# Two attention blocks on one core: narrower guard products, strided scaling, and new due times for the projection jobs

## The chip, the cores and the metric

The kernel runs on one core of a Trainium2 chip. The metric is the device time of the whole program in microseconds (us). The engines are TensorE (PE in the profile, PEld for its weight loads), VectorE (DVE), ScalarE (ACT), GpSimd (POOL) and SyncE (SP, which issues most DMAs). SBUF is the working memory; PSUM takes the matmuls' outputs, in 8 banks of 512 float32 columns for each of 128 partitions.

## What is computed

There are two independent attention blocks over 2048 tokens of width 1024, with 32 heads of 32 channels each. Their outputs stand side by side in an output of 2048 x 2048. Inputs and output are bfloat16.

Block A is plain attention:

```
q, k, v = split(A_x @ A_wqkv)                       # 32 heads x 2048 x 32
p = softmax(q @ k.T / sqrt(32));   a = (p @ v) @ A_wo
```

Block B cuts the tokens into 4 segments of 512. In each segment it mixes causal attention inside the segment with a linear memory of the segments before, by a gate for each head:

```
q, k, v = B_x @ B_wq, B_x @ B_wk, B_x @ B_wv        # 4 segments x 512 tokens
for s in range(4):
    a_dot = softmax(q[s] @ k[s].T / sqrt(32) + causal mask) @ v[s]
    a_mem = phi(q[s]) @ M / (phi(q[s]) . z + 1e-6)  # phi(t) = t + 1 if t > 0 else exp(t)
    o[s] = g * a_mem + (1 - g) * a_dot              # g = sigmoid(beta), one per head
    M += phi(k[s]).T @ v[s];   z += sum(phi(k[s]))
b = o @ B_wo
```

## The kernel before

**Attention.** Heads are worked four at a time: a group g is 4 heads of A (8 groups), and B has 8 such groups j in each segment s, taken in pairs (s, 0) to (s, 3). A unit is 256 query columns of a group of A, or a pair of groups of B. `plan_set` (line 911) writes the logits of four heads into two of three PSUM slots of two banks each (`SLOT_BANKS`): one matmul for each head and 128 keys (line 955). `plan_exp` (1003) lets ACT take the exponential of 1024 logits a partition into a ring of 20 buffers (`P_RING`; line 1034). `round` (1096) multiplies the probabilities by V and by a column of ones (1130 and 1137, the PV rounds), into one accumulator bank. `norm` (1178) turns the sums into reciprocals by `recip_rows` (1144): a 32x32 transpose (1155) brings the sums of a head into one column of every 32, a reciprocal is taken (1165), for B it is scaled by 1 - g (1167), and a second transpose (1169) spreads it again. B's memory denominators go through the same function with 1e-6 added (1162) and a reciprocal in place (1163). For about a quarter of A's key tiles the exponential of one tile in four is a cubic on DVE and POOL instead (`plan_cube`, 979: lines 992, 995, 996, 997).

**Guards.** The exponentials subtract no maximum. Instead a bound on each unit's logits is computed from sums of squares. POOL squares the projected keys and queries (`square`, 1314); `guard_cols` (1321) sums the squares of each head over its channels by a matmul (1327), 512 tokens wide, and takes the maximum over the tokens (1334); `guard_end` (1365) multiplies an identity matrix by that column (1371), spreads it over all partitions by a matmul with ones (1380), takes the maxima for each head (1388) and writes a bias and a flag (1394 to 1405). At the first exponential of a unit with a new guard, ACT's queue waits for the flag, reads it into a register and branches: lines with a bias if the bound was passed, line 1034 without one if not (`run_split`, 521). A guard thus has to be done before its unit's first exponential.

**Jobs.** All else that PE does is cut into jobs: projections of A's keys and queries (`job_KA`, 1508) and values (`job_VA`, `job_V0`), of B's (`job_KB`, 1573; `job_VB`), the memory's products (`job_phi`, `job_mem`, `job_M`, 1583 to 1655), the output products (`job_outA`, `job_outB`) and the guards. Nearly every job uses one PSUM bank, the X bank (bank 6): 8 steps of matmuls (line 595, the helper `mm4`), then a copy out by DVE (line 1304), and only then may the next job open the bank.

**Who sets the order.** The program plans itself before it runs. Each operation is given a duration from a formula in the helpers `dve`, `act`, `pool`, `pe` (578 to 587; `fixed` is its constant part) and a key, the time at which it is wanted. Jobs get a release time r, a due time d and a cost by `add` in `plan_jobs` (1784). `level` (83) spreads them by earliest due time over the stretches where the load is highest, and the time it finds becomes the key. `schedule` (221) then simulates the engines, operation by operation, and the order that comes out is each engine's fixed program. On PE the choice is made by `pick` (294): logits matmuls ("row", urgent) come first once ACT is within `ROW_LEAD` of needing them; among the rest the lowest rank wins:

```python
if x.pvn is not None:
    k = (x.pvn + PV_ROOM - st["opn"]) * PV_T if st["rows"] and x.need - st["opn"] > PV_HOT else -100.0
else:
    k = JOB_AT + JOB_SLOPE * max(min(x.key - st["prog"], 20.0), -20.0)
    k = min(k, DUE_AT + DUE_SLOPE * (x.due - st["prog"]))
```

Here `pvn` is the exponential that a PV round belongs to, `opn` the number of exponentials issued so far, `need` the exponential that waits for the round's buffers, and `prog` the key of the last exponential. A job step that is longer than the slack before the next logits by more than `OVER` is put off (321). DMAs are issued by SP in such an order too, each held behind an exponential near its key; `STEP`, `OT_STEP` and `WOA_STEP` are the distances between the pieces of a load, `RX0` the start of B's first load of tokens, `LEAD_A` and `LEAD_B` the time by which the projections' due time lies ahead of their unit.

**Constants.** `identf` (828, 829), `onesb`, `blk32` (833 to 841) and `maskbd`, a float32 block-diagonal mask of 128x128 (842 to 849), are made by POOL at the start. The mask is scaled by the memory's z into `Zb` (1608) and multiplied with M into `Mb` (1655). The gate's four columns `gc` are made by `beta` (1484 to 1497).

Of the kernel before, what the change touches and what calls it, by code (L numbers as in the profile page):

```python
# [11 lines left out]
P = 128  # L12
# [16 lines left out]
PHI_AT = 7.583  # L29
# [9 lines left out]
BCK = 8.851  # L39
SOON = 0.388  # L40
# [110 lines left out]
ROW_LEAD = 1.148  # L151
# [15 lines left out]
BACKLOG = 2.5  # L167
XR = 11.254
XC = 2.153
STEP = 1.462  # L170
OUT3 = 55.735
OT_STEP = 1.5
WOA_STEP = 2.149
OUT_D = 59.313
# [3 lines left out]
class Prog:  # L178
# [42 lines left out]
    def schedule(self):  # L221
# [31 lines left out]
        def ready_of(o):  # L253
            t = 0.0
            for x in o.deps:
                t = max(t, x.end + x.lat)
# [13 lines left out]
        def opening(o):  # L270
# [5 lines left out]
            return max((x.end + x.lat if x.sched else 1e9 for h in o.halves for x in last[h]), default=0.0)  # L276
# [286 lines left out]
class _Kernel:  # L563
# [101 lines left out]
    def alloc(self):  # L665
# [71 lines left out]
        self.identf = sb("identf", [P, P], dt.float32)  # L737
# [9 lines left out]
        self.dg = sb("dg", [P, 2, P])  # L747
# [71 lines left out]
    def plan_constants(self):  # L819
# [3 lines left out]
        def pool1(f, n=128):  # L823
# [4 lines left out]
        pool1(lambda e: e.memset(self.identf[:, :], 0.0))  # L828
        pool1(lambda e: e.affine_select(self.identf[:, :], self.identf[:, :], pattern=[[-1, P]],
                                        compare_op=ALU.not_equal, fill=1.0, base=0, channel_multiplier=1))  # L830
# [11 lines left out]
        pool1(lambda e: e.memset(self.maskbd[:, :], 1.0))  # L842
# [301 lines left out]
    def recip_rows(self, src, rsrc, n, key, add=None, keep=None, scale=None):  # L1144
# [16 lines left out]
        if add is not None:  # L1161
            self.dve(lambda e: e.tensor_scalar(rv, v, add, None, ALU.add), nb, key, [r2], [rr])
# [3 lines left out]
        if scale is not None:  # L1166
            self.dve(lambda e: e.tensor_scalar(rc[:, 0:nb], rc[:, 0:nb], scale, None, ALU.mult), nb, key, [rr, self.r_g], [rr])  # L1167
# [10 lines left out]
    def norm(self, t, key):  # L1178
# [24 lines left out]
        T2, r2 = self.recip_rows(lsrc, ro, QC, k, keep=keep, scale=self.gc[:, 1, g:g + 1] if kind == "B" else None)  # L1203
# [117 lines left out]
    def guard_cols(self, key, sqs, bank=None, urgent=None):  # L1321
        b = self.xbank() if bank is None else bank

        def mm(e):
            ins = None
            for c, (sq, rs) in enumerate(sqs):
                ins = e.matmul(self.ps[32 * c:32 * c + 32, 512 * b:512 * b + 512], self.blk32[:, :], sq[:, :], start=True,
# [622 lines left out]
```

## Time and profile before

| What | Value |
|---|---|
| Median of 3 runs (range) | 1125.24 us (1122.95 to 1126.01) |
| The profiled execution's own time | 1121.7 us |
| Its span, first to last instruction | 1120.0 us |
| Mean granted TensorE clock | 0.998 |
| HBM read, written | 45.23 MB, 11.67 MB |
| Share of the last chain: ACT, PE, DVE | 48%, 37%, 10% |

The profile is one execution of the program. Its page gives each engine's busy time, its share of the span and its instructions. The view of waits adds up, for an engine and a line, the idle time in front of an instruction by what released it; the releaser is inferred from semaphores, and is that of the semaphore which came last. The order of time lists instructions by start, duration, engine and line, runs of equal ones merged (x8), with the idle time before them in brackets. In every view `out<-in` are the program's tile names: `ps` is PSUM, `P` the probabilities, `T` and `rc` the reciprocals, `cols`, `dg`, `braw`, `bias` and `flags` the guards. A matmul's end is modelled, so PE's busy time is not its work at full rate.

### The profile page before, as it was taken

Reading aid. Unit: us, or ns where it says so; the run is one execution under the profiler, and the core shown is the slowest. Engines: PE = TensorE matmul, PEld = TensorE weight load, DVE = VectorE, ACT = ScalarE, POOL = GpSimd, SP = SyncE. Lnnn points to the kernel's source line nnn. Section 1 sums busy time; section 2 is a strip of 40 time slices with the busy share of each in tenths; the row PEclk is TensorE's granted clock in tenths of the full one; section 3 lists DMA queues with packets and bytes.
Section 4 is the critical chain, followed back from the end, with each engine's and each line's share of the span. In section 5 each row is a group of like instructions: output and inputs, shape, how many; then the busy total and the mean of one; then the engine's idle time right before and its main releaser. Section 6 shows DMA issues by size and latency. Waiting matters only on the chain.

```text
span 1120.0 us, 54777 instructions
## 1 busy us (share of the span) xinstructions
PE 1037.4 (93%) x25064; PEld 554.0 (49%) x25064; DVE 747.3 (67%) x1566; ACT 1068.7 (95%) x1224; POOL 679.3 (61%) x653
## 2 busy tenths in 40 slices
PE   8999999998999989999999998988999989999998
PEld 4456444465444444456445444645545434445544
DVE  3345667855665588868775788688755868775544
ACT  4989999998999999999999999999999989999997
POOL 2215576756586566857575686775856758665431
PEclk9999999999999999999999999999999999999999
DMA  9212350005123230023241230142140460022101
GB/s 197 51 48 46 83 129 15 15 16 120 45 64 91 65 99 17 15 54 81 64 91 55 73 71 8 34 87 60 47 106 27 135 178 3 22 68 78 37 22 54
DMA packets 171096, 71.96 MB, mean 64 GB/s; under 512 B 134768, under 2 KB 169072, under 8 KB 170864
## 3 DMA queue, kind: packets, MB, share of 16 engines
q1 hardware_dynamic: 168496, 67.66, 24.3%
q8 instruction: 197, 3.23, 1.2%
q10 hardware_dynamic: 2368, 0.79, 0.3%
q14 instruction: 35, 0.29, 0.1%
HBM read 45.23 MB, written 11.67 MB: 51 GB/s over the span
## 4 chain that ended last, share of the span: by engine, by line
ACT 48%; PE 37%; DVE 10%; issue 2%; POOL 2%; DMA 1%; ACTq 0%; DVEq 0%
ACT P L1034 47%; PE ps L595 19%; PE ps L955 7%; PE ps L1130 5%; PE ps L1137 5%; DVE PKQ_B L1596 1%; DVE Pc L997 1%; PE ps L1547 1%; DVE Y L992 1%; DVE T L1155 1%; ACT PKQ_B L1591 1%; DVE KQ_B L1304 1%; ACT P L1021 1%; DVE rc L1167 1%; DMA xT_A<-in_A_x_dram 1%
## 5 line engine op out<-in xcount | busy, mean ns | idle before, releaser
L1034 ACT ACTIVATE P<-ps 128x1024 bf16<-128x1024 f32 (+1 forms) x1176 | 1041.0, 1086 | 31.3 <-PE ps L1137 13.4
L1137 PE MATMUL ps<-P,onesb 128*32 128x256 bf16 (+1 forms) x4628 | 297.4, 270 | 0.4 <-issue 0.4
L995 POOL TENSOR_SCALAR Z<-Y 128x512 f32<-128x512 f32 x118 | 184.7, 1566 | 146.6 <-DVE Y L992 146.3
L1130 PE MATMUL ps<-P,V_A 128*32 128x256 bf16 x3860 | 254.6, 274 | 5.4 <-DVE T L1158 1.7
L955 PE MATMUL ps<-KQ_A 32*128 32x256 bf16 x4096 | 203.7, 273 | 26.5 <-ACT P L1034 20.0
L996 POOL TENSOR_TENSOR Z<-Z,Y 128x512 f32<-128x512 f32 x118 | 152.6, 1294 | 4.9
L1137 PEld LDWEIGHTS ps<-P,onesb 128*32 128x32 bf16 x4628 | 129.3, 97 | 36.8 <-issue 12.8
L955 PEld LDWEIGHTS ps<-KQ_A 32*128 32x128 bf16 x4096 | 61.5, 92 | 171.3 <-ACT P L1034 135.0
L595 PE MATMUL ps<-xT_A,W_A 128*32 128x512 bf16 (+1 forms) x2232 | 137.9, 363 | 4.7 <-DVE OT_B L1617 1.1
L595 PE MATMUL ps<-xT_B,W_B 128*32 128x512 bf16 (+1 forms) x2188 | 136.7, 369 | 5.3 <-DVE cols L1334 1.5
L1054 POOL TENSOR_SCALAR_AFFINE_SELECT P<-P 128x768 bf16<-128x768 bf16 (+1 forms) x96 | 78.6, 822 | 92.4 <-ACT P L1034 91.6
L1130 PEld LDWEIGHTS ps<-P,V_A 128*32 128x32 bf16 x3860 | 108.4, 96 | 43.5 <-issue 16.4
L992 DVE TENSOR_SCALAR Y<-ps 128x512 f32<-128x512 f32 x118 | 80.7, 684 | 69.4 <-PE ps L955 67.6
L1318 POOL TENSOR_TENSOR sqA<-KQ_A 128x512 bf16<-128x512 bf16 x61 | 65.5, 1074 | 101.4 <-DVE KQ_A L1304 65.3
L997 DVE SCALAR_TENSOR_TENSOR Pc<-Z,Y 128x512 bf16<-128x512 f32 x118 | 104.3, 884 | 29.4 <-POOL Z L996 25.8
L1318 POOL TENSOR_TENSOR sqB<-KQ_B 128x512 bf16<-128x512 bf16 x64 | 69.6, 1092 | 50.0 <-DVE KQ_B L1304 36.5
L1155 DVE STREAM_TRANSPOSE T<-ps 128x256 f32<-128x256 f32 (+1 forms) x148 | 71.8, 485 | 18.9 <-PE ps L1137 13.0
L595 PEld LDWEIGHTS ps<-xT_A,W_A 128*32 128x32 bf16 x2232 | 52.1, 96 | 55.1 <-issue 18.4
L595 PEld LDWEIGHTS ps<-xT_B,W_B 128*32 128x32 bf16 x2188 | 50.6, 96 | 53.7 <-issue 19.8
L1304 DVE CAST KQ_A<-ps 128x512 bf16<-128x512 f32 x60 | 41.2, 687 | 51.2 <-PE ps L595 50.6
L1169 DVE STREAM_TRANSPOSE T<-rc 128x256 f32<-128x256 f32 (+1 forms) x152 | 72.2, 478 | 2.3
L595 PE MATMUL ps<-Wv_B,xT_B 128*32 128x512 bf16 (+1 forms) x1116 | 69.0, 364 | 4.5 <-DVE V_B L1304 1.5
(104 smaller groups left out, 1323.4 us busy)
## 6 DMA issues: line engine op xcount, KB each, us to landing
Wv_B<-in_B_wv_dram SPq DMA_DIRECT2D x32, 256.0 KB, 3.1
W_B<-in_B_wk_dram SPq DMA_DIRECT2D x32, 256.0 KB, 3.2
W_B<-in_B_wq_dram SPq DMA_DIRECT2D x32, 256.0 KB, 3.8
Wo_B<-in_B_wo_dram SPq DMA_DIRECT2D x32, 256.0 KB, 3.0
out_dram<-outsb SPq DMA_DIRECT2D x56, 128.0 KB, 1.8
W_A<-in_A_wqkv_dram SPq DMA_DIRECT2D x14, 256.0 KB, 3.7
ot_a_scratch<-OTst SPq DMA_DIRECT2D x50, 64.0 KB, 1.7
xT_A<-ot_a_scratch SPq DMA_DIRECT2D x6, 512.0 KB, 5.8
```

Of the source, the lines that this page charges most:

```text
L595: ins = e.matmul(out[r], w[:, r], x, start=start, stop=stop, tile_position=(0, 32 * t), skip_group_check=True)
L955: ins = e.matmul(out, kap, qap, start=st, stop=True, tile_position=(32 * h, 0), skip_group_check=True)
L992: o = self.dve(lambda e: e.tensor_scalar(Y[:, :], src, KAPPA * SCALE, -KAPPA * ROOT, ALU.mult, ALU.add), 512, key - 9.0, [self.bank[bank]] ...
L995: self.pool(lambda e: e.tensor_scalar(Z[:, :], Y[:, :], CUBE_A, None, ALU.add), 512, key - BCK, [rY], [rZ], rate=0.38)
L996: self.pool(lambda e: e.tensor_tensor(Z[:, :], Z[:, :], Y[:, :], ALU.mult), 512, key - BCK, [rY, rZ], [rZ], rate=0.435)
L997: last.append(self.dve(lambda e: e.scalar_tensor_tensor(out=dst, in0=Z[:, :], scalar=CUBE_B, in1=Y[:, :], op0=ALU.add, op1=ALU.mult), 512, ...
L1034: a = self.act(guarded if early else lambda e: e.activation(dst, src, ACT.Exp, scale=SCALE), cols, key, rd, wr, fixed=EXP_FIXED)
L1054: self.pool(lambda e: e.affine_select(v, v, pattern=pat, compare_op=ALU.is_ge, fill=0.0, base=0, channel_multiplier=-1), 2 * nd * P, key + ...
L1130: ins = e.matmul(self.ps[32 * h:32 * h + 32, 512 * obk + q0:512 * obk + q0 + nq], v, p, start=first, stop=last, tile_position=(0, 32 * h), ...
L1137: ins = e.matmul(self.ps[32 * h:32 * h + 32, lcol + q0:lcol + q0 + nq], self.onesb[:, 0:32], p, start=False, stop=last, tile_position=(0, ...
L1155: self.dve(lambda e: e.transpose(T2[:, 0:n], src), n, nk, rsrc, [r2], fixed=0.17)
L1318: self.pool(lambda e: e.tensor_tensor(sq[:, :], src, src, ALU.mult), 512, key, [rsrc], [rs], rate=0.5)
```

## The change

1. **Spread.** `guard_end` no longer scales a 128x128 identity. It copies the column, times `UP`, over 32 columns (`dg`), uses that as the weights, and a constant `pick` of 128x16 as the moving side: 0.125 where partition p belongs to column p // 8. The eight equal rows of a head add up to its value. The output has 16 columns for each column spread, in place of 128, and the maxima are taken over those. There are four matmuls for each column spread.
2. **Token parts.** `guard_cols` gets a width. For B it is 128: the products of the four parts of 128 tokens are added in one PSUM stretch of 128 columns, and the maximum is taken over those. B's bound is then that of sums over four tokens, at least as large as before. A's stays at 512.
3. **Scaling.** In `recip_rows` B's scaling comes ahead of the reciprocal: T's strided column times a new `gc[:, 3]`, the reciprocal of 1 - g, into `rc`, then the reciprocal in place. `maskbd` becomes bfloat16, every second element of a tile of 128x128x2.
4. **Model durations.** Some `fixed` values are new (`Zb`, `Mb`, `zf`, `rc`, `dg`).
5. **Parameters.** Some twenty of the planner's parameters have new values, and each job's due time is shifted by `NUDGE`, a table by class of job (kind, segment or group, pair or half), though not to before its release time. `SAFE` is 0, so it adds nothing.

```diff
-PHI_AT = 7.583
+PHI_AT = 6.978
-BCK = 8.851
-SOON = 0.388
+BCK = 9.626
+SOON = 0.39
-ROW_LEAD = 1.148
+ROW_LEAD = 1.017
-OVER = 1.928
+OVER = 1.64
-PV_T = 1.347
-PV_HOT = 1.189
+PV_T = 1.269
+PV_HOT = 1.702
-JOB_AT = -0.604
-JOB_SLOPE = 0.8
+JOB_AT = 0.555
+JOB_SLOPE = 0.737
-RX0 = 30.552
-LEAD_A, LEAD_B, DUE_AT, DUE_SLOPE = 14.219, 9.124, 2, 0.342
+RX0 = 34.384
+LEAD_A, LEAD_B, DUE_AT, DUE_SLOPE = 14.219, 8.77, 4.982, 0.1
-BACKLOG = 2.5
-XR = 11.254
+BACKLOG = 2.178
+XR = 9.514
-STEP = 1.462
-OUT3 = 55.735
-OT_STEP = 1.5
-WOA_STEP = 2.149
-OUT_D = 59.313
+STEP = 1.785
+OUT3 = 87.197
+OT_STEP = 2.92
+NUDGE = {('KB', 3, 1): 8.43, ('VB', 1, 1): -8.13, ('OB', 0, 0): 8.85, ('OB', 2, 0): 12, ('KB', 1, 0): 7.83, ('OA', 4): -18.13, ('KB', 3, 0): -14.16, ('KA', 5): -2.7, ('KB', 3, 2): 0.67, ('OA', 3): -1.8, ('OA', 5): 0.15, ('VB', 0, 0): -25, ('phi', 3, 1): 6.17, ('KB', 3, 3): -2.7, ('KB', 2, 2): -3.03, ('OA', 0): 0.43, ('VB', 2, 0): 3.71, ('phi', 0, 1): -1.72, ('KB', 1, 1): -2.67, ('phi', 1, 1): 6.71, ('phi', 3, 3): 4.88, ('VB', 1, 0): -3.01, ('OB', 0, 1): 5.6, ('VB', 2, 1): 1.82, ('OB', 3, 0): 0.39, ('VB', 3, 1): -7.84, ('OB', 1, 1): 0.61, ('OB', 1, 0): 4.5, ('KB', 1, 2): -4.13, ('phi', 0, 0): 6.16, ('VB', 0, 1): 9.83, ('OB', 3, 1): -2.58, ('phi', 2, 2): -0.46, ('KB', 2, 1): 4.39, ('VA', 1): 6.19, ('KA', 2): -1.14, ('KA', 6): -6.01}
+SAFE = 0
+WOA_STEP = 3
+OUT_D = 57.959
...
-        self.maskbd = sb("maskbd", [P, P], dt.float32)
+        self.maskbd = sb("maskbd", [P, P, 2])[:, :, 0]
...
+        pool1(lambda e: e.memset(self.pick[:, :], 0.125), 16)
+        for sign, base in ((-8, 0), (8, 7)):
+            pool1(lambda e, sign=sign, base=base: e.affine_select(
+                self.pick[:, :], self.pick[:, :], pattern=[[sign, 16]], compare_op=ALU.is_ge, fill=0.0, base=base,
+                channel_multiplier=1 if sign < 0 else -1), 16)
...
-        if add is not None:
-            self.dve(lambda e: e.tensor_scalar(rv, v, add, None, ALU.add), nb, key, [r2], [rr])
+        if scale is not None:
+            self.dve(lambda e: e.tensor_scalar(rv, v, scale, None, ALU.mult), nb, key, [r2, self.r_g], [rr], fixed=0.15)
+            self.dve(lambda e: e.reciprocal(rc[:, 0:nb], rc[:, 0:nb]), nb * 8, key, [rr], [rr])
+        elif add is not None:
+            self.dve(lambda e: e.tensor_scalar(rv, v, add, None, ALU.add), nb, key, [r2], [rr], fixed=0.15)
...
-        if scale is not None:
-            self.dve(lambda e: e.tensor_scalar(rc[:, 0:nb], rc[:, 0:nb], scale, None, ALU.mult), nb, key, [rr, self.r_g], [rr])
...
+            for lo in range(0, 512, wide):
+                for c, (sq, rs) in enumerate(sqs):
+                    ins = e.matmul(self.ps[32 * c:32 * c + 32, 512 * b:512 * b + wide], self.blk32[:, :], sq[:, lo:lo + wide], start=not lo,
+                                   stop=lo + wide == 512, tile_position=(0, 32 * c), skip_group_check=True)
...
-            self.dve(lambda e, i=i, c=c: e.tensor_scalar(dg[:, i, :], self.identf[:, :], self.cols[:, c:c + 1], UP,
-                                                         ALU.mult, ALU.mult), 128, key, [r, self.r_c], [rdg], fixed=0.25)
+            self.dve(lambda e, i=i, c=c: e.tensor_scalar(dg[:, i, :], self.cols[:, c:c + 1].to_broadcast([P, 32]), UP, None, ALU.mult),
+                     32, key, [r], [rdg], fixed=0.13)
...
-            x = dg[:, 0:n, :].rearrange("p a b -> p (a b)")
-            for t in range(4):
-                r = slice(32 * t, 32 * t + 32)
-                ins = e.matmul(self.ps[r, 512 * b:512 * b + P * n], self.onesb[:, 0:32], x, start=True, stop=True,
-                               tile_position=(0, 32 * t), skip_group_check=True)
+            for i in range(n):
+                for t in range(4):
+                    r = slice(32 * t, 32 * t + 32)
+                    ins = e.matmul(self.ps[r, 512 * b + 16 * i:512 * b + 16 * i + 16], dg[:, i, :], self.pick[:, :], start=not i, stop=True,
+                                   tile_position=(0, 32 * t), skip_group_check=True)
...
-        def add(r, d, c, f):
-            jobs.append((r, d, c, f))
+        def add(r, d, c, f, *tag):
+            jobs.append((r, max(d + NUDGE.get(tag, 0.0), r), c, f))
```

More of the change, by code (lines that the diff above doesn't have):

```diff
@@ L254, in ready_of @@
             t = 0.0
+            job = SAFE if o.eng == "PE" and o.urgent is None else 0.0
             for x in o.deps:
-                t = max(t, x.end + x.lat)
+                t = max(t, x.end + x.lat + (job if x.eng in ("DVE", "POOL") else 0.0))
             for x in o.order:
@@ L275, in opening @@
                 return 1e9
-            return max((x.end + x.lat if x.sched else 1e9 for h in o.halves for x in last[h]), default=0.0)
+            return max((x.end + x.lat + SAFE if x.sched else 1e9 for h in o.halves for x in last[h]), default=0.0)
         def heat(t, span):
@@ L1877, in plan_jobs @@
                 if c < 6:
-                    add(r, min(r + OUT_D, st["A", 7, 7]), OUT, lambda key, row=row, hf=hf: self.job_outA(row, hf, key))
+                    add(r, min(r + OUT_D, st["A", 7, 7]), OUT, lambda key, row=row, hf=hf: self.job_outA(row, hf, key), "OA", c)
                     continue
```

55 lines of the change are left out of this document (25 added, 30 removed).

## The prediction

> **What bounds the kernel now.** I read the page's busy times first, then the waits of ScalarE, then the order of time around its longest wait. From the page:
>
> ```profile
> PE 1037.4 (93%) x25064; PEld 554.0 (49%) x25064; DVE 747.3 (67%) x1566; ACT 1068.7 (95%) x1224; POOL 679.3 (61%) x653
> ```
>
> ScalarE (ACT) works 1068.7 of 1120.0 us, so its idle time, 51.3 us, is all that a new order of the work can win. What ended that idle time (total, times, longest):
>
> ```profile
> ACT P L1034 <- PE ps L1137: 13.4, 13, 3.6
> ACT KQ_A L1465 <- PE ps L595: 8.3, 1, 8.3
> ACT P L1034 <- PE ps L955: 8.1, 15, 1.2
> ACT P L1034 <- PE ps L595: 7.3, 2, 6.5
> ACT P L1021 <- DVE bias L1397: 3.6, 1, 3.6
> ACT KQ_B L1777 <- PE ps L595: 2.9, 1, 2.9
> ```
>
> The first line is the ring of probability buffers: an exponential waits until the PV matmuls (L1130, L1137) have emptied its buffers. The third is logits that came late (L955). The second and fifth are the start, before the first exponential at 15.27 us, the sixth the end. The fourth is one wait of 6.5 us, and its releaser is misnamed; the order of time shows the true one:
>
> ```profile
> 889.05 0.68 DVE L1304 CAST KQ_A<-ps 128x512 bf16<-128x512 f32 x1
> ...
> 894.70 0.40 PE L955 MATMUL ps<-KQ_A 32*128 32x256 bf16 x8
> ...
> 895.34 1.91 PE L595 MATMUL ps<-xT_B,W_B 128*32 128x512 bf16 x32
> ...
> 898.05 0.29 PE L1380 MATMUL ps<-dg,onesb 128*32 128x256 bf16 x4 [0.36 <-DVE KQ_B L1304]
> ...
> 900.61 0.15 DVE L1405 SCALAR_TENSOR_TENSOR flags<-braw,flags 128x1 int32<-128x1 f32 x1
> ...
> 901.24 5.26 ACT L1034 ACTIVATE P<-ps 128x1024 bf16<-128x1024 f32 x6 [6.50 <-PE ps L595]
> ```
>
> The logits were there at 895.10; what came at 900.76 was the flag of A's group 7, and 0.48 us later ACT went on. Its last projection was evicted at 889.05, so the guard took 11.7 us, because a projection of B's (L595, x32) got the one spare PSUM bank between the guard's two steps. No other flag is late: I set each flag's end beside the first logits of its unit, and the margins of the other groups of A are 41 to 81 us, of B's pairs 24 to 111 us, but for B's segment 3, pair 1: flag 908.62, logits 914.6, margin 6.0 us.
>
> By stretches, ACT idles 19.1 us in 0 to 80, 18.6 in 80 to 840, 6.5 in 840 to 902, and 0.3 in 902 to 1112.
>
> **The change part by part.**
>
> *Guards, VectorE.* The instructions on the guards' columns (tile cols; ns min/median/max):
>
> ```profile
> L1334 DVE TENSOR_REDUCE cols<-ps x34: 648/691/693, 13.0 to 942.9; 128x1 f32<-128x512 f32 x34
> L1371 DVE TENSOR_SCALAR dg<-identf,cols x34: 190/454/1372, 13.8 to 944.8; 128x128 bf16<-128x128 f32 x34
> L1388 DVE TENSOR_REDUCE cols<-ps x27: 266/291/426, 14.5 to 947.6; 128x2 f32<-128x128 f32 x20, 128x2 f32<-128x256 f32 x7
> ```
>
> B's 16 guards reduce 128 columns in place of 512: from a mean of 685 to about 284 ns (L1388's mean at 128 columns), 16 x 0.40 = 6.4 us. The second reduce goes from 128 and 256 columns to 16 and 32; its means by shape, 284 and 417 ns, give 1.04 ns a column, so about 167 and 184 ns: 20 x 0.12 + 7 x 0.23 = 4.0 us. The 34 scalings of dg shrink from 128 to 32 elements; unobstructed ones take 0.28 us, so at most 34 x 0.1 = 3 us. In all about 13 us of VectorE, which is idle a third of the time. On ACT's path lie only the guards of the start (flag at 15.3, and at 24.56, 0.68 us before ACT's 1.70 us wait ends): about 0.12 us of reduce and 0.1 of dg in each: **-0.5 us**.
>
> *Guards, TensorE.* B's sums become 16 matmuls of 128 columns for 4 of 512: the same columns, 12 more weight loads. In the order of time four loads follow in 0.11 us, so 0.44 us for 0.40, and at most 0.2 us x 16 = 3.2 us of an engine that is 93% busy. The spreads stream fewer columns with up to four more loads: nothing. The bank is held about 0.4 us less for each guard of B; late flags are one in 27, so I cost that at 0, with both ends at 1 us.
>
> B's bound grows at most fourfold. Its tokens are of size 0.05 and its weights of 0.05/32, so a key channel is about 0.0025 (32 x 0.05 x 0.05/32) and a head's 32 squares sum to 0.0002, far from FREE = 0.125: no flag goes up, and ACT stays on line 1034.
>
> *Constants.* The identity's memset and select (pitch 0.43 and 0.35 us on POOL) become a memset and two selects of 16 columns (blk's selects come every 0.27 us): the same 0.8 us, and POOL is done at 9.2, while the first guard product starts at 12.5. One reciprocal of 0.2 us is added for beta, beside the one at 109.5 us on VectorE, and read from 164 us on: 0.
>
> *Strided operands.* The reciprocals and scalings of rc (tile rc):
>
> ```profile
> L1165 DVE RECIPROCAL rc<-T x128: 143/182/302, 66.9 to 1113.4; 128x8 f32<-128x8 f32 x128
> L1167 DVE TENSOR_SCALAR rc<-rc,gc x64: 187/490/1325, 164.3 to 1009.6; 128x8 f32<-128x8 f32 x64
> L1162 DVE TENSOR_SCALAR rc<-T x24: 152/166/1261, 396.4 to 996.2; 128x16 f32<-128x16 f32 x24
> ```
>
> The order of time explains L1167's spread: about 0.22 us when POOL is idle; when it works, usually until 24 to 31 ns after POOL's instruction, 0.58 us on average. The reciprocals never wait so. In the new order the scaling reads a strided column of T and the reciprocal follows; the count stays. L1162 already has that form (strided T to rc) and waits too: 1.26 us at 624.50, ending 30 ns after POOL's L996 at 625.73; 8 of its 24 met a working POOL, and 7 ended 28 to 30 ns after it. So I take 0. The other end is that nothing waits: 64 x (0.54 - 0.22) + 24 x (0.45 - 0.24) + 34 x (0.51 - 0.28) = 33 us of VectorE, of which the late logits (8.1 us) bound what ACT gains; I keep -6 for that case.
>
> No row shows a two-byte source of stride 2 (the new mask) or one element read 32 times (dg). [...]
>
> *Order of PE's jobs.* This is the large part. A job of the X bank ranks JOB_AT + JOB_SLOPE x lead, a PV round (pvn + 3.546 - opn) x PV_T. For a job on time the two are equal when PV lags 3.99 exponentials before (0.604/1.347 + 3.546) and 3.11 after (3.546 - 0.555/1.269). PV thus goes first about 0.9 exponential, 0.8 us, sooner. PV_HOT from 1.189 to 1.702 compares whole numbers: no effect. Shortening each of the 13 ring waits by up to 0.8 us gives 9.0 us at most (the longest, 3.6 us at 60.4, follows 1.96 us of V projections that PE did before PV); 0 at least, since what PE did in its place returns. I take the middle: **-4.5**.
>
> OVER from 1.928 to 1.64 lets a job overrun due logits by 0.29 us less, 15 waits x 0.29 = 4.3 at most; ROW_LEAD 0.13 us shorter costs 15 x 0.13 = 2.0: **-2**, between +2 and -4.
>
> *Due times by class.* KA of group 7 has no nudge. B's KB(3,1), three of whose jobs ran at 831 to 838 ahead of it and whose fourth was evicted at 893.3, is due 8.43 us later (+0.35 from LEAD_B), KB(3,0) 14.16 earlier, OB(2,0) 12 later. So KB(3,1) should let A's group 7 and its guard pass: the flag needs to come 6.5 us sooner, less than the 10 us that the three jobs held (831.2 to the next class's 841.2). That removes 6.5; next late is PE, 95% busy from 902 on, which did B's jobs during the wait and now does them beside exponentials. I take **-5.5**, between 0 and -6.5.
>
> *Loads.* WoA's pieces come 3.0 for 2.15 us apart and OT's 2.9 for 1.5, so SP's queue gets room among them for W_B, whose query half landed in 4.8 us between 860 and 906 against 3.8 over the run. Stores of out and OTst wait for VectorE and POOL, not for the queue. STEP and RX0 start B's loads up to 4 us later; the first pair's margin of 27 us covers it, and without it 4 us would be lost. 0.
>
> **Sum.** -0.5 - 4.5 - 2 - 5.5 = -12.5 us from the profiled execution's 1121.7 (span 1120.0), so 1109.2. The median of the runs is 1125.24, 3.5 above that execution: 1112.7, **1113 us**.
>
> **Rivals.**
> - *Slower: B's pair (3,1) takes the late flag's place.* Its guard has 6.0 us of margin and its due time moves by 8.8: if the job moves as far, ACT waits 2.8 us, and if A's group 7 starts 5.5 us sooner, 8.3. It decides once the flag moves over 6.0 us against the logits. With A's wait unremoved and no gain elsewhere 1125.2 + 2.8 = 1128; if the logits' wait for ROW_LEAD (+2) and the start (+4) add, up to 1134. For it: the smallest margin in the list. Against it: a due time moves a job only as far as the load around it allows. 22%.
> - *Nothing gained: the stalls change place.* PE is at 93 to 95%; what it does not do before an exponential it does before a later one. 1122 to 1128: 10%.
> - *Strided operands free VectorE of POOL.* 1113 - 6 = 1107, with the ring waits' full gain 1102. Against it: L1162. 14%.
> - *The guard alone or the ring alone improves:* 1119 to 1121. 8%.
>
> **Chances.** My forecast, 1107 to 1119, has 46%. Faster by over 0.3% (about what a measurement of this kernel can tell from no change), under 1121.9: 46 + 14 + 8 = 68%; within it 10%; slower 22%. The range cuts the ends of the slower rival and of the strided one: 1101 to 1130, about 8 in 10.
>
> **What would show it.** Right: the flag of A's group 7 more than 0.5 us ahead of its logits, and no ACT wait above 2 us between 80 and 1112; ring waits below 9 us; scaling of rc still ending some 28 ns after POOL's instruction. Wrong: an ACT wait just after a flag of B's pair (3,1), or ring waits above 13; a mean of rc's scaling near 0.2 us would mean that strides do free it. The forecast also fails if the start before 80 us grows beyond 19.1 us of idle.

## The result, and the profile after

The changed kernel takes 1121.66 us (median of 22 runs, 1119.28 to 1126.58) against 1125.03 us of the kernel before (22 runs); the ratio is 0.9973, with an interval of 0.9963 to 0.9982. That is 3.4 us less, where 12.5 us were forecast. The profiled execution took 1119.28 us, its span is 1117.6 us.

The page's busy times of after. The engines do nearly the same work (VectorE 3 us less than before, 744.2 for 747.3). ScalarE's busy time is the same; its share rises because the span is shorter:

```profile
PE 1039.4 (93%) x25336; PEld 555.5 (50%) x25336; DVE 744.2 (67%) x1567; ACT 1068.5 (96%) x1224; POOL 675.6 (60%) x654
```

What ended ScalarE's idle time in after (total, times, longest). In order: the ring, the flag of A's group 7 (again under a wrong releaser's name), the start, late logits, the start, the end:

```profile
ACT P L1039 <- PE ps L1142: 11.3, 15, 2.9
ACT P L1039 <- PE ps L598: 8.9, 1, 8.9
ACT KQ_A L1473 <- PE ps L598: 8.2, 1, 8.2
ACT P L1039 <- PE ps L960: 4.5, 10, 1.1
ACT P L1026 <- PE ps L598: 3.5, 1, 3.5
ACT KQ_B L1786 <- PE ps L598: 2.9, 1, 2.9
```

Ring waits fell from 13.4 to 11.3, late logits from 8.1 to 4.5. The wait for the flag, which was to go, grew from 6.5 to 8.9. Its place in the order of time of after:

```profile
884.85 0.68 DVE L1310 CAST KQ_A<-ps 128x512 bf16<-128x512 f32 x1
...
886.29 0.40 PE L960 MATMUL ps<-KQ_A 32*128 32x256 bf16 x8
...
891.19 1.91 PE L598 MATMUL ps<-xT_B,W_B 128*32 128x512 bf16 x32 [0.95 <-DVE rc L1173]
...
893.89 0.22 PE L1388 MATMUL ps<-pick,dg 128*32 128x16 bf16 x8 [0.79 <-DVE KQ_B L1310]
...
895.22 0.15 DVE L1413 SCALAR_TENSOR_TENSOR flags<-braw,flags 128x1 int32<-128x1 f32 x1
895.86 1.02 ACT L1039 ACTIVATE P<-ps 128x1024 bf16<-128x1024 f32 x1 [8.90 <-PE ps L598]
```

The unit's first logits stand 8.4 us earlier than before (886.29 against 894.70), the flag's end only 5.4 (895.37 against 900.76). As before, projections of B's, 32 matmuls each, take the bank ahead of the guard's first step and between its two (887.1 and 891.19), and the guard takes 10.5 us from the last copy to the flag, against 11.7. ScalarE was free for group 7 at 886.96, 7.8 us earlier than before (894.74), and went on 5.4 us earlier (895.86 against 901.24): 2.4 of the 7.8 were waited away there. Of the 5.4, 3.0 were lost behind the flag, 2.0 of them at the end and 1.0 at a ring wait at 932 (last section).

In the two profiled executions ScalarE's idle time went from 51.3 to 49.1 us: -2.1 ring, -3.6 late logits, -0.6 in the guards of the start, **+2.4** flag, **+2.0** at the end (below), -0.3 elsewhere.

The instructions changed in after, by tile cols and by tile rc (ns min/median/max):

```profile
L1342 DVE TENSOR_REDUCE cols<-ps x34: 246/664/692, 12.9 to 952.5; 128x1 f32<-128x512 f32 x18, 128x1 f32<-128x128 f32 x16
L1379 DVE TENSOR_SCALAR dg<-cols x34: 126/181/1245, 13.6 to 952.8; 128x32 bf16<-128x32 f32 x34
L1396 DVE TENSOR_REDUCE cols<-ps x27: 115/174/192, 14.4 to 955.1; 128x2 f32<-128x16 f32 x20, 128x2 f32<-128x32 f32 x7
```

```profile
L1167 DVE TENSOR_SCALAR rc<-T,gc x64: 129/440/1310, 160.9 to 1003.8; 128x8 f32<-128x8 f32 x64
```

They cost about what was forecast for them. The scaling from a strided column still reaches 1310 ns.

**A measure for traces.** ScalarE's 61st exponential starts anywhere from 76.0 to 80.6 us in the profiled executions, by when the first loads landed (last section). So spans are compared from that exponential to the end: 1042.49 us before, 1041.55 after, 0.9 us less. This compares one execution with one; the times are medians of several, and the two measures can differ by 2 to 3 us.

### The profile page after: what moved, and what is told of

It is laid out like the page before. It is cut to its first block, busy times and chain, and to the rows that moved or that the text cites. A ratio compares the mean times of both kernels' runs of the same rounds, so it can differ in the third digit from the quotient of the medians.

```text
span 1117.6 us, 55335 instructions
## 1 busy us (share of the span) xinstructions
PE 1039.4 (93%) x25336; PEld 555.5 (50%) x25336; DVE 744.2 (67%) x1567; ACT 1068.5 (96%) x1224; POOL 675.6 (60%) x654
## 3 DMA queue, kind: packets, MB, share of 16 engines
q8 instruction: 199, 3.26, 1.3%
## 4 chain that ended last, share of the span: by engine, by line
ACT 43%; PE 42%; DVE 11%; issue 2%; POOL 2%; ACTq 0%; DVEq 0%; POOLq 0%
ACT P L1039 41%; PE ps L598 22%; PE ps L960 8%; PE ps L1135 6%; PE ps L1142 5%; DVE Pc L1002 1%; DVE T L1160 1%; DVE PKQ_B L1605 1%; DVE rc L1167 1%; DVE Y L997 1%; ACT PKQ_B L1600 1%; PE ps L1556 1%; ACT P L1026 1%; DVE T L1163 1%; DVE outsb L1310 1%
## 5 line engine op out<-in xcount | busy, mean ns | idle before, releaser
L1039 ACT ACTIVATE P<-ps 128x1024 bf16<-128x1024 f32 (+1 forms) x1176 | 1041.2, 1078 | 27.4 <-PE ps L1142 11.3
L1000 POOL TENSOR_SCALAR Z<-Y 128x512 f32<-128x512 f32 x118 | 182.1, 1544 | 155.7 <-DVE Y L997 140.8
L1002 DVE SCALAR_TENSOR_TENSOR Pc<-Z,Y 128x512 bf16<-128x512 f32 x118 | 110.7, 938 | 26.3 <-POOL Z L1001 19.5
L1310 DVE CAST KQ_B<-ps 128x512 bf16<-128x512 f32 x64 | 44.0, 687 | 46.4 <-PE ps L598 45.0
```

The costliest lines, as they stand in the source:

```text
L1000: self.pool(lambda e: e.tensor_scalar(Z[:, :], Y[:, :], CUBE_A, None, ALU.add), 512, key - BCK, [rY], [rZ], rate=0.38)
L1002: last.append(self.dve(lambda e: e.scalar_tensor_tensor(out=dst, in0=Z[:, :], scalar=CUBE_B, in1=Y[:, :], op0=ALU.add, op1=ALU.mult), 512, ...
L1039: a = self.act(guarded if early else lambda e: e.activation(dst, src, ACT.Exp, scale=SCALE), cols, key, rd, wr, fixed=EXP_FIXED)
```

## The experiments

"The order" is each engine's fixed list of instructions. Between before and after about half of the rows of TensorE's list differ (equal neighbours merged, counted in the traces). Where an edit keeps the order, the text says so.

**1, 2. Take away the flag's wait.** The guard of A's group 7 is computed, but its bias and flag go to a column that no exponential reads; that unit's check is left out.

```diff
-self.guard_end(key + 0.2, [self.colA[(g, 0)], self.colA[(g, 1)]], 1, [g % 2])
+self.guard_end(key + 0.2, [self.colA[(g, 0)], self.colA[(g, 1)]], 1, [g % 2 if g < 7 else 40])
```

> The kernel before, with the exponentials of A's group 7 not waiting for its guard (the guard is computed, but its bias and flag go to a spare column, and the group uses those of group 5; that part of the computation is left out). Theory 1, the late flag alone sets when ACT goes on there: the 6.5 us wait goes and little comes in its place, 1125.0 - 6.5 = 1118.5 us (1117 to 1120). Rival, PE is the bound there and the wait only hides its backlog: the time stays within 2 us of before, 1123 to 1125, and new waits for logits or for the ring of probabilities appear after 895 us.

> The changed kernel with the same edit (group 7's guard is computed and not waited for). Theory 1: the changed order brings ACT to group 7 8.4 us earlier than before, and 3.0 us of that is lost again in a flag wait that grew from 6.5 to 8.9 us; without it 1121.7 - 8.9 = 1112.8 us (1111 to 1115), so the change's gain over before, both unhooked, is about 5.7 us in place of 3.4. Rival, PE's backlog: 1118 to 1121, with new waits after 886 us.

Before without the wait: 1117.4 us, ratio 0.9945 (0.993 to 0.996). After without it: 1113.11, 0.9905 (0.9891 to 0.992). By the ratios that is 6.2 us under before and 7.6 under after, so the flag does set the time. It is not the price of the wait alone. The edit also moves TensorE's list from 895 us on in the one and from 887 in the other, and run 2's list lacks 2.0 us that after loses at its end (runs 14, 15). In the traces, from the 61st exponential, the gains are 4.0 and 5.6 us (2.0 of the 5.6 is that end); ring and late logits take a part back (ring 15.8 us for 13.4 in run 1; in run 2 ring 13.7 for 11.3 and late logits 9.2 for 4.5). That run 2 lands on the forecast's 1113 is thus partly luck. The place was right; the change does not remove the wait.

**3, 4. The code alone, the parameters alone.**

> The changed guards, scaling, mask and model durations with the planner parameters of before and no nudges. Theory: VectorE's 10 us or so saved are not on ACT's path, so 1124 to 1126 us, the same as before, and the 3.4 us come from the parameters. Rival, the shorter guards give the gain by themselves: 1121 to 1122.5 us.

> The code of before with the new parameters and nudges. Theory, the order makes the difference: 1121 to 1123 us, with ring waits near 11 us, late logits near 4.5 us in place of 8.1, and the flag of A's group 7 still the longest wait. Rival, the parameters only fit the new code: 1125 us or slower.

The new code with the old parameters and no nudges: 1129.4, 1.0057 (1.0043 to 1.0071). The old code with the new parameters and nudges: 1141.01, 1.0145 (1.0122 to 1.0169). Both theories missed; the rival of the second, 1125 us or slower, held. Neither part brings what the two bring together, and the losses stand at other places. The code alone has its flag wait of 6.0 us, a wait of 6.0 at 792 for GpSimd's list that no other kernel has (no flag is written between 765 and 813), and 2.2 at its end. The parameters alone have the flag 12.2 us late and a longer ring. ScalarE's waits of the code alone:

```profile
ACT P L1039 <- PE ps L598: 6.0, 1, 6.0
ACT P L1039 <- POOL sqB L1324: 6.0, 1, 6.0
```

**5, 6. Another order of the units**, so that group 7 starts one unit later.

```diff
-PAIR = ((6, 0), (6, 1), (6, 2), (7, 0), (7, 1), (7, 2), (6, 3), (7, 3), ...
+PAIR = ((6, 0), (6, 1), (6, 2), (6, 3), (7, 0), (7, 1), (7, 2), (7, 3), ...
```

> The kernel before with one unit of A moved: (6, 3) goes ahead of (7, 0), so that group 7 starts one unit (about 14 us) later; nothing is left out. Theory 1, the late flag: it is then in time and the wait of 6.5 us goes without a new one, about 1118 us (1116 to 1120), as with the wait taken out (1117.4). Rival, the jobs behind group 7 are late whatever the order of units: another flag or the ring takes its place, 1122 to 1126.

> The changed kernel with the same swap of units; nothing is left out. Theory 1: the flag wait of 8.9 us goes, about 1113 us (1111 to 1116), near the 1113.1 of the unhooked one. Rival: 1118 to 1122, with a new wait for a flag of B's segment 3 or for the ring.

1136.71, 1.0131 (1.0108 to 1.0153), and 1125.7, 1.0019 (1.0006 to 1.0032): both missed. The wait for the flag is gone from both, and the ring takes more than that back, 400 us and more ahead of the edit (the longest waits are at 422 and 460). The first line of ScalarE's waits, of before with the edit and of after with it:

```profile
ACT P L1034 <- PE ps L1137: 32.3, 25, 7.5
```

```profile
ACT P L1039 <- PE ps L1142: 28.2, 24, 5.3
```

**7. The scaling moved, planned anew.** B's scaling goes into the copy out of PSUM beside it (in after these copies, L1163, take 378 to 415 ns, all 123 of them, where the scalings take 129 to 1310), so 64 operations of VectorE fall away.

```diff
-self.dve(lambda e: e.tensor_copy(T2[:, n:2 * n], keep), n, nk, rsrc, [rk])
+self.dve(lambda e: e.tensor_scalar(T2[:, n:2 * n], keep, scale, None, ALU.mult), n, nk, [*rsrc, self.r_g], [rk])
```

> The changed kernel with B's scaling moved into the copy of the numerators out of PSUM, which is not stretched by POOL's work: the 64 scalings of rc (33.8 us of VectorE, 0.53 us each) go and the copy becomes a multiply. Theory 1, VectorE's waits for POOL are not what paces ACT, and what is won ahead of group 7 is lost at its flag: 1119.5 to 1122 us, VectorE's busy time about 33 us less. Rival, the waits of VectorE for POOL cost ACT time: 1113 to 1118.

1132.76, 1.008 (1.0064 to 1.0096). VectorE's busy time fell by 28 us, and the kernel is 11 us slower than after, by 22.0 us of ring waits and a flag wait of 13.7. Again about half of the rows of TensorE's list had moved. Runs 3 to 7 suggest a second theory: an edit that reaches the planner makes it deal much of the order anew, and the deal moves the time by more than the edit. So the next edits keep the order.

**8. The same scaling, with the order kept.** The 64 scalings become reciprocals in their place, and the 64 reciprocals behind them write a spare tile.

> After's kernel with the order of every engine kept and one group of VectorE operations replaced: the 64 scalings that end 25 to 28 ns behind a GpSimd instruction (33.8 us busy in all, the fast form 0.129 us) become reciprocals of the same place of the chain, and the scaling itself moves into the copy out of PSUM beside it (same outputs; one more small operation's result is left unused). Theory 2 (the time is set by the order the planner wrote, and VectorE's waits for GpSimd lie under slack): 1119.7 to 1122.5, ratio to the kernel before 0.995 to 0.998, the same as after. Rival (the strided operands were to free these 64 operations and their stall of some 25 us is what the change missed): 1116 or less, ratio 0.992 or less. The 64 operations' busy time should fall from 33.8 to under 15 us in either.

1117.27, 0.9949 (0.9934 to 0.9964); from the 61st exponential 2.7 us less than after. Those 64 operations take 11.5 us for 33.9, the copies 28.6 for 25. What the strided operands failed to free was thus worth between 2 and 3 us, not the 6 that the prediction kept as the other end. The same edit is 11 us slower when it is planned anew (run 7).

**9. The guard's instructions alone, in before's order.** All the guard's edits of the change, no other, and old planning sizes, so the order is before's.

> Before's kernel with the order of every engine kept and only the guard's instructions changed to those of after (B's sums in four parts of 128 columns, so reductions of 128 columns for 512; a product of 16 columns; a second reduction of 16 columns for each head set). Theory 1 and 2 together: with the order held, what is gained is what these instructions save ahead of A's group-7 flag, 0.22 us of the second reduction, 0.44 us of the reduction that stands between it and the flag and up to 0.3 us of the broadcast, and 0.3 us at the start: 1122.7 to 1124, ratio 0.998 to 0.9995. Rival (the instructions are worth what the change brought, 3 us and more, and the order costs nothing): ratio 0.9975 or less. Rival (the code itself makes the loss of the code-alone run, +5): ratio 1.002 or more.

1118.31, 0.9961 (0.9946 to 0.9975): the guard's instructions alone give 4.4 us, more than the whole change; 3.6 us in the traces from the 61st exponential. Flag and ring hardly move (6.3 and 12.8 us). The expectation of 1 us missed, so both theories lacked something.

**10, 11. B's sums alone**, in before's order, and taken back in after's order.

```diff
+for lo in range(0, 512, wide):          # before + this, wide = 128 for B
+    ... start=not lo, stop=lo + wide == 512 ...
```

> Before's kernel with the order of every engine kept and only B's guard sums in four parts of 128 columns (the product by the identity, its broadcast of 128 columns and the second reduction stay as in before). The run with all of the guard's instructions was 4.4 us faster. Theory: VectorE's time taken off goes as 16 x 0.45 = 7 us for the sums to 34 x 0.23 + 34 x 0.15 = 13 us for the rest, and the waits it ends at are ring waits, which both reach alike: a third of the gain, 1 to 2 us, ratio 0.998 to 0.999. Rival (the 0.69 us reductions alone hold VectorE long enough to make the normalizing operations late): nearly all of it, ratio 0.9955 to 0.9972.

> After's kernel with the order of every engine kept, and B's guard sums over 512 columns again in place of four parts of 128 (16 reductions of 0.69 us for 16 of some 0.25 us; the 16-column product stays). Theory 3 (the guard's shorter instructions are what the change gained, through many small waits, and the new order gained nothing): 1.5 to 4 us slower than after, ratio 0.9985 to 1.001. Rival (in after's order these instructions stand under slack, and the order is the gain): same as after, ratio 0.9963 to 0.9982.

Before with the sums: 1118.93, 0.9952 (0.9939 to 0.9966). After without them: 1124.52, 1.0009 (0.9996 to 1.0022). The first expectation missed and its rival held; the second held. By the times, the sums are the whole gain of the guard in before's order (5 us), and after without them is no faster than before. In the traces, from the 61st exponential, they are worth 2.7 and 3.5 us (5.4 and 4.0 by the times). Of the 2.7, 1.5 stand at 258, as in run 9, where before has a stall with no guard near (last section). Of the 3.5, 1.2 is one stretch from 752 to 755 in which TensorE's granted clock was 0.50. That leaves 1.2 and 2.3 us.

One way in which a reduction that ScalarE never waits for can do this is seen at one guard of B. Before: the sums' bank is not free until the reduction ends, the next entry of TensorE's list is a projection that needs it, and the logits stand behind that in the list.

```profile
408.48 0.68 DVE L1334 TENSOR_REDUCE cols<-ps 128x1 f32<-128x512 f32 x1
...
409.22 0.61 PE L595 MATMUL ps<-xT_B,W_B 128*32 128x512 bf16 x8 [0.52 <-DVE cols L1334]
...
409.77 0.40 PE L955 MATMUL ps<-KQ_A 32*128 32x256 bf16 x8
```

The same place in the kernel of run 9:

```profile
406.23 0.28 DVE L1337 TENSOR_REDUCE cols<-ps 128x1 f32<-128x128 f32 x1
...
406.66 0.62 PE L595 MATMUL ps<-xT_B,W_B 128*32 128x512 bf16 x8 [0.20 <-DVE cols L1337]
```

The projection starts 0.43 us behind the reduction's start, not 0.74, and TensorE idled 0.20 us for it in place of 0.52. At this guard the loss is TensorE's alone: in both kernels the weight loads of the logits behind it then waited for ScalarE (0.42 us before, 0.73 in run 9). Over the run, TensorE's largest waits for a guard's reduction, by its view of waits, before, before with the sums (run 10), after, and after without the sums (run 11):

```profile
PE ps L595 <- DVE cols L1334: 3.3, 7, 0.8
PE ps L595 <- DVE cols L1388: 1.3, 3, 0.7
```

```profile
PE ps L595 <- DVE cols L1335: 2.0, 5, 0.8
PE ps L595 <- DVE cols L1389: 1.3, 3, 0.7
```

```profile
PE ps L598 <- DVE cols L1396: 2.1, 5, 0.5
PE ps L598 <- DVE cols L1342: 1.2, 4, 0.6
```

```profile
PE ps L598 <- DVE cols L1341: 2.9, 10, 0.6
PE ps L598 <- DVE cols L1395: 2.8, 5, 1.3
```

With the smaller lines that wait for a guard's reduction it is 5.5, 5.3, 3.3 and 5.7 us. The bank can thus carry the 2.3 us in after's order, but not the 1.2 in before's, where this sum fell by 0.2. There is a rival, which run 10's expectation named: the same 0.4 us stand in VectorE's own list, ahead of its transposes and copies, and TensorE's waits for `T` fell from 7.0 to 5.4 us in run 10. The edit shortens both at once, and no run separates them. That the sums are worth it is shown; by which of the two ways is not.

**12. Chain the guard.** In after, the two steps of group 7's guard hold the bank together.

```diff
+self.colA[(7, 1)] = self.guard_cols(key - 12.0, self.sq71, urgent=True)
+self.xr.grp.chain = True
+self.guard_end(key - 11.9, [self.colA[(7, 0)], self.colA[(7, 1)]], 1, [1], bank=X_BANKS[0], urgent=True)
```

> After's kernel with A's group-7 guard put into one chain: the sums of its second half, its broadcast and its flag hold the one shared PSUM bank without a projection job of B between them, and go ahead of other work for it (78 of 4567 rows of TensorE's list differ). Theory 1 (A's group-7 flag paces and is late because B's guard and a projection take the bank between its two steps): the flag comes 3 to 5 us sooner, ScalarE's wait for it falls from 8.9 to 4 to 6 us, the time to 1116 to 1119, ratio 0.992 to 0.995. Rival (B's group (3,1), now later by the same 3 to 5 us of a margin of 10, or its ring, takes the place): 1120 to 1123, ratio 0.996 to 0.999.

1116.05, 0.9936 (0.9918 to 0.9954), as expected in size, but for other reasons. The wait fell from 8.9 to 6.1 us, just short of what was expected, 1.0 of this came back as late logits right behind it, and 2.0 us came from the end of ScalarE's list, which this edit shifts (runs 14, 15). 78 of 4567 rows moved.

**13. Group 7's projections earlier.**

```diff
+if tag == ("KA", 7):
+    t = max(t - 15.0, r)
```

> After's kernel with the eight projection jobs of A's group 7 planned 15 us earlier (not before their release; 304 of 4567 rows of TensorE's list differ). Theory 1: A's group-7 flag comes 6 to 12 us sooner, the 8.9 us wait for it goes to under 3 us, the time to 1113 to 1118, ratio 0.990 to 0.9945, the same as with the wait taken away. Rival (the output jobs that they pass are late in their place, or the ring waits elsewhere grow): 1119 to 1124, ratio 0.995 to 1.000, with a new wait of over 4 us beside.

1118.83, 0.9962 (0.995 to 0.9974): the rival's figure. The flag stands 1.1 us ahead of its logits, the wait is gone (0.5 left), but ScalarE comes to group 7 5.4 us later than in after (892.4 against 887.0), held at 863, 876 and 884, and the ring grows. Part of this may be the clock: it was 0.50 from 881.1 to 891.3, so the longest of these waits, 3.1 us up to 887.5, lies under it, and all ten executions of this kernel have a mean of 0.993 to 0.995. What the projections passed and what the clock took is not separated. ScalarE's waits:

```profile
ACT P L1039 <- PE ps L1142: 14.8, 16, 3.1
...
ACT P L1039 <- PE ps L960: 6.5, 13, 1.6
```

**14, 15. The end.** In after, ScalarE's two last waits ended at 1115.03 and 1117.09, though all other engines were done by 1115.07; in before the two were 0.08 us apart. Between them the trace has one transfer, of instructions:

```profile
q14 instruction: 1, 0.01, 1.2%
```

One run spares ScalarE these waits, one puts four small activations at the head of its list, which moves the list's end.

```diff
-for s in final_sems:
+for s in final_sems if e != "ACT" else ():
```

```diff
-self.act(lambda e: e.activation(self.warm[:, :], self.warm[:, :], ACT.Exp), 1500, key,
+self.act(lambda e: [e.activation(self.warm[:, k:k + 1], self.warm[:, k:k + 1], ACT.Exp) for k in range(5)][-1], 1500, key,
```

> The changed kernel with ACT no longer waiting for the last output DMAs (the other four engines still do). Theory: in the changed kernel's profile ACT's second final wait is 2.05 us behind its first, with an instruction DMA between them, and the other engines are done 2.4 us before the span ends; so 1119.5 to 1120 us. Rival, the end is set by the outputs' landing: 1121.5 to 1122, no change.

> After's kernel with four more one-column activations on ScalarE ahead of its first work, so that its instruction list is four longer in front of its end; nothing else moves. Theory (the 2.0 us between the last two semaphore waits of ScalarE's list is the fetch of the list's next block, which falls between them by where the block ends): the gap goes from 2.06 us to under 0.2 us, the span falls by about 2.0 us, ratio to the kernel before 0.9945 to 0.996. Rival (something else is waited for there, the output's DMAs): the gap stays, ratio 0.9965 to 0.998.

Without the waits: 1119.73, 0.9967 (0.9954 to 0.9981). The 2.0 us did not go: they stand between ScalarE's drain at 1114.83 and its last semaphore at 1116.88. With the list shifted: 1119.86, 0.9967 (0.9949 to 0.9985). There the two waits are 0.08 us apart, and from the 61st exponential the execution is 3.5 us shorter than after (2.0 at the end, 1.0 at the ring wait at 932). The gap stands in after and in runs 3, 8, 11 and 13 as well (2.0 to 2.2 us), at another place in run 14, and in none of the other lists. So it goes with the position in the list; the times of these two runs alone could not have told, as neither median is clear of after's.

**16. Both repairs**: run 12 with run 8.

> Two of the runs together: after's kernel with A's group-7 guard in one chain, and with the 64 scalings taken into the copies out of PSUM (same outputs). If the two add up, 4.2 + 2.7 us below after: 1113 to 1116 against 1124, ratio 0.990 to 0.9925. Rival (both shorten the same waits, or the chain's gain was the end of ScalarE's list alone): ratio 0.993 to 0.9955.

1115.0, 0.9913 (0.9899 to 0.9926): by the times they add up, 9 us below before and faster than both kernels. As in run 12, 2.0 of this is the end.

**17, 18. Nudges.** One that moves the order is taken out, then all.

```diff
-('KB', 3, 3): -2.7,
```

```diff
-NUDGE = {('KB', 3, 1): 8.43, ...}
+NUDGE = {}
```

> After's kernel without one of its 37 nudges, the 2.7 us by which B's last group's projection is planned earlier. It is one of nine that change the order when taken out alone (the nudge of group (3,1), on which the forecast was built, changes not one row), and this one moves 1533 of 4567 rows of TensorE's list from about the 579th on. Theory 2 (any input of the planner re-deals the order, and the time moves by several us without regard to what was edited): over 2 us from after, more likely slower, ratio 1.000 to 1.012. Rival (the time follows the edited job alone, which has 30 us of slack): ratio 0.996 to 0.9985, as after.

> After's kernel without any of its nudges (1971 of 4567 rows of TensorE's list move). Theory 2: the nudges as a whole are worth what was found by trying orders, not what each does to its own job: 3 to 15 us slower than after, ratio 1.000 to 1.011, with the loss in ring waits and in one or two late flags. Rival (they are worth little): ratio 0.996 to 0.999.

1122.74, 0.9995 (0.9982 to 1.0008), and 1126.49, 1.0023 (1.001 to 1.0036). To take out a nudge of 2.7 us, on a job with 30 us of slack, costs some 2.5 us; all of them together are worth 5.6. Both lists lack the 2.0 us at the end, so what their order loses is more. In both the flag wait is only 4.0 us, and the ring doubles. First line of ScalarE's waits without any nudge:

```profile
ACT P L1039 <- PE ps L1142: 22.0, 19, 4.5
```

## Why the prediction was wrong, point by point

**The step that failed: "KB(3,1) should let A's group 7 and its guard pass", -5.5.** Planned with that one nudge at 0, or at 14.43, after has row for row the same lists on all five engines: this due time decides nothing. Of the 37 nudges, 8 change TensorE's list when taken out alone (run 17's expectation says nine). I read a due time's shift as a job's shift, but `level` spreads jobs by the load around them. I also had the wrong jobs. The planned lists, laid beside the traces, show whose projections stand there. In after all four of pair (3,1) are copied out at 823.2 to 833.2 us, far ahead of the guard; the fourth, at 893.3 before, came 60 us sooner although its due time moved later. The projection between the guard's two steps is pair (3,2)'s in both kernels (copied out at 897.3 before, at 893.1 in after), and in after the one ahead of the first step is (3,2)'s too (889.1). So (3,1) was out of the way, and the flag still waited: the logits came 8.4 us sooner, the flag 5.4, and the wait grew from 6.5 to 8.9 us in place of going. Runs 1 and 2 show that it had a price: 4.0 and 3.6 us in the traces, 6.2 and 5.6 by the times, run 2 without the 2.0 at the end.

**Guards: -0.5, measured -3.6 to -5.** The instruction durations were right (128 columns: 246 to 293 ns for 284 forecast; the second reduction 174 median for 167 to 184). The term that was mis-sized is "the bank is held about 0.4 us less for each guard of B; ... I cost that at 0, with both ends at 1 us". I asked only who waits for a flag, and not what stands behind the reduction in TensorE's and VectorE's lists; which of the two it is stays open (runs 10, 11). It is not all guard, either: of the 3.6 us in run 9's trace, 1.5 stand at one exponential at 258.0, where before has a stall of TensorE with no guard near (last section). The forecast of 13 us less work for VectorE did not come out in its total, which fell by 3.1; the instructions named did shrink as costed.

**Ring -4.5, logits -2: measured -2.1 and -3.6**, together 5.7 for 6.5. But run 9, with before's parameters, has 2.2 of the logits' gain and 0.6 of the ring's. So the parameters' part is some 2.9, and runs 3, 4, 17 and 18 say that it belongs to this set of parameters with this code, not to any one of them.

**What the sum lacked: the end, +2.0**, runs 14 and 15.

**Right.** The strided operands free nothing: scalings that met a working GpSimd mostly end 25 to 28 ns behind its instruction (mean 567 ns for 321 when it is idle). The same shows where the prediction had no row of before: dg, one element read 32 times, and `Zb`, from the mask of stride 2. With GpSimd at work their means are 495 and 500 ns, without it 171 and 258. No flag of B's pair (3,1) was late, its margin grew from 6.0 to 10.1 us, so the slower rival's mechanism did not come up; run 13 may show its kind, with other work. The start went to 24.68 us from 25.24, as costed.

**Together.** With the order of before, the guard gives 3.6 us in the traces. With everything, 0.9 (1042.49 to 1041.55). The 2.7 us between are 2.0 at the end of ScalarE's list and 0.7 net for the order dealt anew, less than the 1.0 of the ring wait at 932: what the new order won in ring and logits, the flag took back.

There is a rival that no run tries, the clock. The mean granted clock of after's 22 executions is 0.9955, that of the 95 executions of before that were taken beside the experiments 0.9970. After's executions at 0.997 and 0.998 took 1119.7 to 1120.5 us, those at 0.992 to 0.994 took 1123.2 to 1126.6. The difference of 0.0015 is 1.7 us of a span of 1118, an estimate of what the clock may hold back.

What stays open is which of the parameters puts pair (3,2) between the guard's steps. Runs 12 and 13 free the flag by force and gain 4.2 and 1.2 us by the ratios, the first with the 2.0 at the end in it.

## What to carry to other kernels

A parameter of a planner is to be followed into the planned order, not into the quantity that it names: build the list, compare the rows, and if they are the same, its price is zero. To price an instruction in such a kernel, hold the order and change it alone; planned anew, the same edit cost 11 us that gave 2.7 with the order kept. And an operation whose result nobody on the critical engine waits for can still count: by the bank that it holds, or by what stands behind it in its own engine's list.

## What the runs showed of the hardware

**Stalls that look like late code.** Two stalls look like waits for instructions. The traces show their places and the transfers of instructions beside them; that the one made the other is an inference. In after 199 transfers of instructions move 3.26 MB in all (queue q8), 16 KB each and one for 127 of TensorE's 25336 matmuls, and 36 smaller ones move 0.29 MB (q14), 8 KB each. The first stall is the 2.0 us at the end of after: the one transfer between the two waits is of q14, and four more instructions ahead removed the gap (runs 14, 15). ScalarE's list has a branch just ahead of these waits (1112.17 in after), but in before, too (1116.56), where the two are 0.08 us apart; that the branch has a part in it was not shown. The second is TensorE's. In before it waited for nothing that the profile shows:

```profile
257.34 0.29 PE L595 MATMUL ps<-Wv_A,xT_A 128*32 128x256 bf16 x4 [1.36 <-issue]
```

This is the 5565th matmul recorded. Run 1 has the same list there and lost 0.41 us at the same matmul; after and the seven runs with its list there lost 0.5 to 1.1 us at their 5564th. The next such stalls stand 127 to 129 matmuls further on, about the step of q8's transfers. So the place belongs to the list, and the length changes from one execution to the next: the 1.5 us that runs 9 and 10 have over before at 258 are partly chance. From 251.5 to 255 the DMA engines were 90% busy or more, with a transposing load among their work; that this held up TensorE's code is a guess that no run tried.

**The granted clock fell to 0.50 behind some stretches in which TensorE was partly idle.** In after the granted clock was 0.50 from 925.0 to 931.8, with TensorE 1.77 to 2.00 us busy in each 2 us. Ahead of it TensorE was busy for 2.13 us of 3.50 (921.5 to 925), by modelled ends. The 20 traces have 26 such stretches between 70 and 1100 us. Each lasts 3.4 us or two or three times that, and in the 3.4 us ahead of each TensorE was busy for 36 to 61% of the time. Not every stretch like that is followed by one (56% at 744 in after, and no fall). The ring wait at 932 lies just behind the fall; in runs 8, 14 and 15, with TensorE's order the same, that exponential comes 0.6 to 1.0 us sooner. Columns: stretch, its length, busy time (instructions) of the engines, granted clock, DMA:

```profile
920.00:925.00 5.00, 3.63 (x100) 1.70 (x92) 4.76 (x13) 5.00 (x8) 5.00 (x7) 1.00 0.26 58
925.00:927.00 2.00, 1.77 (x28) 0.78 (x28) 2.00 (x7) 2.00 (x4) 2.00 (x2) 0.50 0.61 124
...
929.00:931.00 2.00, 2.00 (x40) 0.78 (x32) 1.97 (x4) 1.87 (x3) 2.00 (x4) 0.50 0.00 0
```

They lie at other places in other executions (752 in run 11, 893 in run 12), and one kernel's times spread by up to 8 us (run 15, 1116.5 to 1124.4). **The start** is another part of that spread: TensorE waited 0.60 us for the load of xT_A at 16.2 in after, 2.72 at 18.9 in run 15's kernel.
